# Sliding-window attention beside a GEGLU: three DMA queues by role, zero columns in front of v, a masked product, and an earlier x load

## The chip, the cores and the metric

The kernel runs on one core of a Trainium2 chip. The metric is the device time of one execution in microseconds (us). TensorE does matrix products into PSUM, VectorE and ScalarE work elementwise, GpSimd fills and prepares, and SyncE issues DMAs. DMAs can be issued from SyncE, from ScalarE and from GpSimd; each of the three has a queue of its own onto the core's 16 DMA engines.

## What is computed

x is 2048 x 512 in bfloat16. It is normalised over its rows, and the result xn goes two ways. One is attention with 32 heads of 16 columns, where each token looks at itself and at seven tokens before it, two apart; places before the first token are masked. The other is a GEGLU feed-forward network of width 1792. Their product, behind a SiLU, is added to x.

```python
qkv = xn @ wqkv                              # q, k, v: 32 heads x 16
idx = pos[:, None] - arange(8)[None, :] * 2  # tokens s, s-2, ... s-14
logits = einsum(q, k[idx]) * scale; logits = where(idx >= 0, logits, -1e9)
s = einsum(softmax(logits), v[idx]) @ wo
g = silu((gelu(xn @ w_gate) * (xn @ w_up)) @ w_down)
return x + s * g
```

## The kernel before, in words

The tokens are cut into four blocks j of 512. For each block the kernel normalises four tiles of 128 tokens (`layer_norm`: statistics L285 and L286, L317 the normalisation, all on VectorE; the reciprocal root for blocks 1 to 3 on GpSimd, L307 and L310), transposes them on TensorE (L333), and copies them into xnT (L339 on ScalarE, L341 on VectorE). `qkv` multiplies by wqkv in twelve column groups (L376), each into one of four PSUM buffers of ring "f"; ScalarE copies each to SBUF: q (L389), k (L391) and v (L396, tile vst, four buffers). A vst goes to DRAM at once, into vT_dram (L442, a DMA of SyncE), since the attention wants v in another layout: `load_values` reads it back (L467) as v_arr, with 32 heads x 4 offsets on the partitions. A block has two halves of four such DMAs each, so eight gathers; v_arr has three buffers. For block 0 the columns before the first token don't exist, so a GpSimd memset fills them (L461) and the DMA leaves them out.

`scores` multiplies q by shifted k on VectorE (L488, eight products a block), TensorE sums over the head's columns (L501), ScalarE takes the exponential (L513); in block 0 GpSimd memsets put zeros where a token has no predecessor (L518). `values` multiplies by v_arr (L598, eight products a block) and sums on TensorE (L612). `ffn_pair` computes gate and up (L659), GELU (L669) and their product (L676); `out_tile` does w_down (L713), wo (L701), the SiLU, the gate, the residual and the store (L737).

The order is fixed when the kernel is built. Every piece of work is a task with an engine, an estimated duration, what it depends on, which ring buffers it takes and frees, and a priority. The class Order places one task after another, always the one that could start first by these estimates (priority breaks ties), and so writes one order for each engine, which then executes its instructions strictly in that order. `x_there` and `w_there` are the estimated landing times of x and of the thirds of wqkv. TensorE's large products (`add_main`) are one chain.

DMAs before: SyncE loads half of block 0's x, the thirds of wqkv (L197) and x of blocks 1, 2, 3 (L201), then issues the stores of v, the gathers of v and the output stores, all in one queue. ScalarE loads the other half of block 0's x. GpSimd loads the four other weights (L802) in 14 DMAs, each batch behind the rstd of a block.

Of the kernel before, what the change touches and what calls it, by code (L numbers as in the profile page):

```python
# [9 lines left out]
ALU = mybir.AluOpType  # L10
AF = mybir.ActivationFunctionType
BF16 = mybir.dt.bfloat16
F32 = mybir.dt.float32

P = 128
H = 32
DH = 16
W = 8
PAD = 16
TQ = 512  # L20
HALO = 2 * (W - 1)
# [12 lines left out]
ACT1 = 0.62  # L34
# [9 lines left out]
class Order:  # L44
# [15 lines left out]
    def add(self, eng, dur, fn, deps=(), prio=0.0, takes=(), frees=(), func=None, opens=None, closes=None):  # L60
        t = Task()
        t.eng, t.dur, t.fn, t.prio = eng, dur, fn, prio
        t.deps = [d if isinstance(d, tuple) else (d, HOP) for d in deps if d is not None]
        t.takes, t.frees, t.func, t.opens, t.closes = takes, frees, func, opens, closes
        t.end = None
        t.seq = len(self.tasks)
        self.tasks.append(t)
        return t
# [61 lines left out]
def kernel(  # L130
# [11 lines left out]
    nc = tc.nc  # L142
    B, S, D = A_x.shape
    DF = B_w_gate.shape[1]
    NC = D // P
    NF = DF // P
    NJ = S // TQ
    TPB = TQ // P
    NT = S // P
    VL = TQ + 8  # L150
# [6 lines left out]
    cpool = pool("cpool", 1)  # L157
# [12 lines left out]
    dram = pool("dram", 1, space=bass.MemoryType.DRAM)  # L170
# [10 lines left out]
    add = order.add  # L181
# [5 lines left out]
    wo_sb = wpool.tile([P, NC, D], BF16, name="wo_sb")  # L187
    wg_sb = wpool.tile([P, NC, DF], BF16, name="wg_sb")
    wu_sb = wpool.tile([P, NC, DF], BF16, name="wu_sb")
    wd_sb = wpool.tile([P, NF, D], BF16, name="wd_sb")  # L190
    wqkv_v = A_wqkv.rearrange("(k p) n -> p k n", p=P)

    for t in range(TPB):
        eng = nc.sync if t % 2 == 0 else nc.scalar
        eng.dma_start(out=x_sb[:, t, :], in_=x2d[t * P : (t + 1) * P, :])  # L195
    for i in range(3):
        nc.sync.dma_start(  # L197
            out=wqkv_sb[:, :, i * D : (i + 1) * D], in_=wqkv_v[:, :, i * D : (i + 1) * D]
        )
    for j in range(1, NJ):  # L200
        nc.sync.dma_start(  # L201
            out=x_sb[:, j * TPB : (j + 1) * TPB, :],
            in_=x2d[j * TQ : (j + 1) * TQ, :].rearrange("(t p) d -> p t d", p=P),
        )
    x_there = [3.2, 3.5, 3.8, 4.1] + [9.5] * 4 + [11.5] * 4 + [13.5] * 4
    w_there = [6.0, 7.0, 8.0]


    warm = cpool.tile([P, TQ], BF16, name="warm")
# [45 lines left out]
    for q in range(4):  # L255
# [2 lines left out]
            in_=fold4[32 * q : 32 * (q + 1), :, :],  # L258
        )

    xnT = cpool.tile([P, NC, S], BF16, name="xnT")
    stats = cpool.tile([P, NT, nc.vector.BN_STATS_DIM], F32, name="stats")
    mv = cpool.tile([P, NT, nc.vector.BN_AGGR_DIM], F32, name="mv")
    rstd = cpool.tile([P, NT, 1], F32, name="rstd")
    vT_dram = dram.tile([D, S], BF16, name="vT_dram")
    tiles = {}


    warm_ps = psa.tile([P, TQ], F32, name="warm_ps", tag="a")
# [5 lines left out]
    copied = {}  # L275
    rstd_done = {}
# [121 lines left out]
    def qkv(j):  # L398
        for which in range(3):
            mms = []  # L400
            if j == 0:
                for half in range(2):
                    for c in range(NC):
                        ts = (2 * half, 2 * half + 1)
                        mms.append(
                            add_main(
                                2 * MM,
                                lambda c=c, half=half, which=which: qkv_mm(
                                    0, which, c, half * TQ // 2, (half + 1) * TQ // 2
                                ),  # L410
                                deps=[copied[t] for t in ts] + [(w_there[which], 0.0)],
                                takes=[("f", ("qkv", 0, which, c))] if half == 0 else [],
                            )
                        )
                mms = mms[NC:]
            else:
                for c in range(NC):
                    mms.append(
                        add_main(
                            4 * MM,  # L420
                            lambda c=c, which=which: qkv_mm(j, which, c, 0, TQ),
                            deps=[copied[t] for t in range(j * TPB, (j + 1) * TPB)],
                            takes=[("f", ("qkv", j, which, c))],
                        )
                    )
            for c in range(NC):
                takes = []
                if which == 0 and c == 0:
                    takes = [("q", j)]
                if which == 2:  # L430
                    takes = [("vst", (j, c))]
                e = add(
                    "act", ACT1, lambda c=c, which=which: qkv_evacuate(j, which, c), deps=[mms[c]],
                    prio=-0.5, takes=takes, frees=[("f", ("qkv", j, which, c))],
                )
                if which == 0:
                    q_ready[j] = e
                elif which == 1:
                    k_ready[j] = e
                else:  # L440
                    def store(c=c):
                        nc.sync.dma_start(  # L442
                            out=vT_dram[c * P : (c + 1) * P, j * TQ : (j + 1) * TQ],
                            in_=tiles["vst", j, c][:],
                        )

                    st = add("sp", 0.6, store, deps=[e], prio=-1.0, frees=[])

                    v_stored[j] = add(("dma", j, c), 2.6, lambda: None, deps=[(st, 0.0)], frees=[("vst", (j, c))])

    v_ready = {}

    def load_values(j, half):
        def fn():
            v_arr = vapool.tile([P, DH // 2, VL], BF16, name="v_arr")
            tiles["va", j, half] = v_arr
            for w4 in range(4):
                start = j * TQ - HALO + 2 * w4
                skip = max(0, -start)
                if skip:  # L460
                    nc.gpsimd.memset(v_arr[32 * w4 : 32 * (w4 + 1), :, 0:skip], 0.0)  # L461
                src = bass.AP(
                    tensor=vT_dram.tensor,
                    offset=vT_dram.offset + half * (DH // 2) * S + start + skip,
                    ap=[[S * DH, H], [S, DH // 2], [1, VL - skip]],
                )
                nc.sync.dma_start(out=v_arr[32 * w4 : 32 * (w4 + 1), :, skip:VL], in_=src)  # L467

        issue = add("sp", 2.2, fn, deps=[v_stored[j]], prio=0.0, takes=[("va", (j, half))])
        v_ready[j, half] = add(("dma", "va", j, half), 7.5, lambda: None, deps=[(issue, 0.0)])  # L470


# [3 lines left out]
    def scores(j, prio):  # L476
        exps = []
        for w2 in range(2):
# [30 lines left out]
            def expo(w2=w2):  # L509
                if w2 == 0:  # L510
                    tiles["attn", j] = atpool.tile([P, 2, TQ], BF16, name="attn", tag="attn")
                attn = tiles["attn", j]
                nc.scalar.activation(out=attn[:, w2, :], in_=tiles["L", j, w2][:], func=AF.Exp)  # L513
                if j == 0:
                    for w4 in range(4):
                        n = HALO - 2 * (w4 + 4 * w2)
                        if n > 0:
                            nc.gpsimd.memset(attn[32 * w4 : 32 * (w4 + 1), w2, 0:n], 0.0)  # L518

            ps = []  # L520
            for c in range(NC):
# [10 lines left out]
                "pe", COL16, reduce, deps=[ps[-1]], prio=-0.5, takes=[("a", ("L", j, w2))],  # L532
                frees=[("pr", ("S", j, w2, c)) for c in range(NC)],
            )
            exps.append(
                add(
                    "act", ACT1, expo, deps=[r], prio=-0.6, func="exp",
                    takes=[("attn", j)] if w2 == 0 else [], frees=[("a", ("L", j, w2))],
                )
            )  # L540

        def sums():
            s_ps = psa.tile([P, P], F32, name="sum_ps", tag="a")
# [30 lines left out]
            tiles["b", j] = atpool.tile([P, TQ], BF16, name="b_sb", tag="b_sb")  # L574
            nc.scalar.activation(out=tiles["b", j][:], in_=tiles["b_ps", j][:], func=AF.Copy)

        s = add("pe", 0.4, sums, deps=[(e, 0.5) for e in exps], prio=-0.4, takes=[("a", ("sum", j))])
        r = add("dve", 1.15, recip, deps=[s], prio=-1.5, frees=[("a", ("sum", j))])
        b = add("pe", 0.3, spread_back, deps=[r], prio=-0.4, takes=[("a", ("b", j))])
        b_ready[j] = add("act", ACT1, b_copy, deps=[b], prio=-0.6, frees=[("a", ("b", j))])  # L580
# [203 lines left out]
            add(("dma", "out", t, cs.start), 2.0, lambda: None, deps=[(st, 0.0)], frees=[("sg", t)] if end else [])  # L784


    def load_weights(j, prio):
        pieces = []
        if j == 1:
            v = B_w_gate.rearrange("(k p) n -> p k n", p=P)  # L790
            pieces = [(wg_sb[:, k, :], v[:, k, :]) for k in range(NC)]
        elif j == 2:
            v = B_w_up.rearrange("(k p) n -> p k n", p=P)
            pieces = [(wu_sb[:, k, :], v[:, k, :]) for k in range(NC)]
        else:

            v = A_wo.rearrange("(h g e) n -> e h g n", h=H, g=NC, e=4)
            pieces = [(wo_sb[32 * e : 32 * (e + 1), :, :], v[e]) for e in range(4)]
            v = B_w_down.rearrange("(k p) n -> p k n", p=P)
            pieces += [(wd_sb[:, k : k + 7, :], v[:, k : k + 7, :]) for k in range(0, NF, 7)]  # L800
        for o, i in pieces:
            add("pool", 1.0, lambda o=o, i=i: nc.gpsimd.dma_start(out=o, in_=i), deps=[rstd_done[j]], prio=prio)  # L802


    for j in range(NJ):
        layer_norm(j)
    for j in range(1, NJ):
        load_weights(j, 1.0 + j)
    for j in range(NJ):
        qkv(j)  # L810
    order.freed["h", "wqkv"] = 0.0
    for j in range(NJ):
        for half in range(2):
# [40 lines left out]
```

## Time and profile before

| what | us |
|---|---|
| median of 3 runs | 247.5 (246.55 to 248.46) |
| profiled execution | 246.81 |
| its span, first to last instruction | 245.1 |
| TensorE busy in the span | 229.6 |
| VectorE busy | 157.2 |
| ScalarE busy | 109.4 |
| GpSimd busy | 20.2 |

The profile is of one execution. Engines are called PE (TensorE), PEld (its weight loads), DVE (VectorE), ACT (ScalarE), POOL (GpSimd) and SP (SyncE); a q behind the name is the engine's queue, where DMAs are issued. L376 is line 376 of the kernel. Times are us from the start of the span unless marked ns. The span's 40 slices are 6.13 us each.

### The profile page before, as it was taken

What the parts mean: (1) busy time and instruction counts of PE and PEld (TensorE: products, weight loads), DVE (VectorE), ACT (ScalarE), POOL (GpSimd) and SP (SyncE); (2) the same over time, 40 slices, a digit from 0 to 9 for tenths busy, and PEclk for the clock granted to TensorE, in tenths of its full rate; (3) what the DMA queues carried; (4) which work ended last, traced back from release to release, by engine and by line L of the source; (5) the groups of instructions that cost most, each with busy time, mean ns of one, the idle gap of its engine ahead of it and who ended that gap; (6) DMA issues with size and microseconds to landing.
All of it is one profiled execution on the core that took longest, in us unless ns stands there. A gap on an engine that the chain in (4) does not pass through costs nothing.

```text
span 245.1 us, 3478 instructions
## 1 busy us (share of the span) xinstructions
PE 229.6 (94%) x1336; PEld 106.5 (43%) x1360; DVE 157.2 (64%) x232; ACT 109.4 (45%) x163; POOL 20.2 (8%) x58
## 2 busy tenths in 40 slices
PE   7879999819999999999999999999999999999992
PEld 2667543303444443444444444444444444444441
DVE  4699999934999999999998332233432333443131
ACT  2445567225784479671723341083233143335100
POOL 6057751000000000000000000000000000000000
PEclk9999999967999999999999999999999999999999
DMA  6929979959999800007300000100000100000001
GB/s 197 354 75 312 355 218 250 205 137 199 236 219 220 172 0 3 0 23 163 79 0 3 0 0 21 43 24 0 0 0 4 43 21 21 3 0 0 21 23 43
DMA packets 18529, 22.60 MB, mean 92 GB/s; under 512 B 1424, under 2 KB 17424, under 8 KB 18512
## 3 DMA queue, kind: packets, MB, share of 16 engines
q1 hardware_dynamic: 16912, 16.08, 27.3%
q0 software_dynamic: 1312, 6.03, 7.6%
q10 hardware_dynamic: 288, 0.26, 0.3%
q8 instruction: 10, 0.16, 0.3%
q14 instruction: 7, 0.06, 0.1%
HBM read 18.17 MB, written 4.19 MB: 91 GB/s over the span
## 4 chain that ended last, share of the span: by engine, by line
PE 86%; DMA 7%; DVE 3%; SPq 1%; issue 1%; ACT 1%; DVEq 0%; ACTq 0%
PE u_ps L659 20%; PE y_ps L713 20%; PE g_ps L659 20%; PE qkv_ps L376 13%; PE s_ps L701 6%; DMA vT_dram<-vst 3%; DMA x_sb<-in_A_x_dram 3%; PE L_ps L501 3%; PE O_ps L612 3%; DVE stats L285 2%; PE tr_ps L333 1%; SPq L197 1%; DVE mv L286 1%; SPq L195 0%; PE sum_ps L547 0%
## 5 line engine op out<-in xcount | busy, mean ns | idle before, releaser
L676 DVE TENSOR_TENSOR hT<-gl,u_ps 128x512 bf16<-128x512 bf16 x56 | 38.3, 686 | 36.6 <-PE u_ps L659 34.8
L659 PE MATMUL u_ps<-xnT,wu_sb 128*128 128x512 bf16 x220 | 57.0, 379 | 0.3
L659 PE MATMUL g_ps<-xnT,wg_sb 128*128 128x512 bf16 x217 | 56.5, 379 | 0.4 <-issue 0.2
L669 ACT ACTIVATE gl<-g_ps 128x512 bf16<-128x512 f32 x56 | 33.3, 597 | 49.8 <-PE g_ps L659 43.2
L376 PE MATMUL qkv_ps<-xnT,wqkv_sb 128*128 128x512 bf16 (+1 forms) x234 | 46.1, 344 | 7.5 <-ACT vst L396 6.3
L713 PE MATMUL y_ps<-wd_sb,hT 128*128 128x512 bf16 x217 | 50.3, 379 | 0.4
L598 DVE TENSOR_TENSOR pv<-attn,v_arr 128x2048 bf16<-128x2048 bf16 x32 | 37.8, 1220 | 7.1 <-PE L_ps L501 6.6
L488 DVE TENSOR_TENSOR prod<-q_sb,k_sb 128x2048 bf16<-128x2048 bf16 x32 | 37.6, 1220 | 0.0
L659 PEld LDWEIGHTS <-wg_sb 128*128 128x128 bf16 x224 | 21.6, 98 | 27.2 <-issue 1.7
L376 PEld LDWEIGHTS <-wqkv_sb 128*128 128x128 bf16 x240 | 22.7, 99 | 24.7 <-issue 10.9
L659 PEld LDWEIGHTS <-wu_sb 128*128 128x128 bf16 x224 | 21.5, 98 | 27.0 <-issue 1.7
L713 PEld LDWEIGHTS <-hT 128*128 128x128 bf16 x224 | 21.7, 98 | 26.2 <-issue 0.4
L727 DVE TENSOR_TENSOR sg<-sil,s_ps 128x512 bf16<-128x512 bf16 (+1 forms) x17 | 11.0, 655 | 34.2 <-PE s_ps L701 22.9
L724 ACT ACTIVATE sil<-y_ps 128x512 bf16<-128x512 f32 x16 | 9.6, 597 | 43.8 <-PE y_ps L713 43.8
L701 PE MATMUL s_ps<-wo_sb,o_sb 128*128 128x512 bf16 (+1 forms) x68 | 16.4, 366 | 0.0
L396 ACT ACTIVATE vst<-qkv_ps 128x512 bf16<-128x512 f32 x16 | 9.0, 599 | 15.8 <-DMA vT_dram<-vst 8.3
L285 DVE BATCH_NORM_STATS2 stats<-x_sb 128x6 f32<-128x512 bf16 x16 | 10.8, 673 | 3.7 <-DMA x_sb<-in_A_x_dram 3.7
L391 ACT ACTIVATE k_sb<-qkv_ps 128x512 bf16<-128x512 f32 x16 | 9.2, 599 | 4.6 <-PE qkv_ps L376 4.6
L389 ACT ACTIVATE q_sb<-qkv_ps 128x512 bf16<-128x512 f32 x16 | 8.9, 602 | 5.0 <-PE qkv_ps L376 5.0
L701 PEld LDWEIGHTS <-o_sb 128*128 128x128 bf16 x68 | 6.6, 98 | 7.2
L623 ACT ACTIVATE o_sb<-O_ps 128x1024 bf16<-128x1024 f32 x8 | 8.2, 1022 | 2.1 <-PE O_ps L612 1.5
L669 ACT ACT_TABLE_LOAD x7 | 9.0, 1283 | 0.1
(56 smaller groups left out, 116.6 us busy)
## 6 DMA issues: line engine op xcount, KB each, us to landing
v_arr<-vT_dram SPq DMA_DIRECT2D x24, 260.0 KB, 5.5
vT_dram<-vst SPq DMA_DIRECT2D x16, 128.0 KB, 6.3
out_dram<-sg SPq DMA_DIRECT2D x15, 128.0 KB, 1.7
wg_sb<-in_B_w_gate_dram POOLq DMA_DIRECT2D x4, 448.0 KB, 4.9
wu_sb<-in_B_w_up_dram POOLq DMA_DIRECT2D x4, 448.0 KB, 9.2
wd_sb<-in_B_w_down_dram POOLq DMA_DIRECT2D x2, 896.0 KB, 9.7
wqkv_sb<-in_A_wqkv_dram SPq DMA_DIRECT2D x3, 512.0 KB, 6.2
x_sb<-in_A_x_dram SPq DMA_DIRECT2D x3, 512.0 KB, 8.8
```

The lines of the kernel that those rows point to most:

```text
L285: nc.vector.bn_stats(out=stats[:, t, :], in_=x_sb[:, t, :])
L376: nc.tensor.matmul(tiles["qkv", j, fo][:, lo:hi], lhsT=wqkv_sb[:, dk, fo * P : (fo + 1) * P], rhs=xnT[:, dk, j * TQ + lo : j * TQ + hi], s ...
L391: nc.scalar.activation(out=k_sb[:, c, PAD + j * TQ : PAD + (j + 1) * TQ], in_=ps[:], func=AF.Copy)
L488: nc.vector.tensor_tensor(out=prod[:], in0=tiles["q", j][:, c, :].unsqueeze(1).to_broadcast([P, 4, TQ]), in1=kwin, op=ALU.mult,)
L598: nc.vector.tensor_tensor(out=pv[:], in0=tiles["attn", j][:, w2, :].unsqueeze(1).to_broadcast([P, 4, TQ]), in1=tiles["va", j, half][:, 4 * ...
L659: nc.tensor.matmul(ps[:], lhsT=w[:, dk, fc * P : (fc + 1) * P], rhs=xnT[:, dk, j * TQ : (j + 1) * TQ], start=(dk == 0), stop=(dk == NC - 1),)
L669: nc.scalar.activation(out=tiles["gl", j, fc][:], in_=tiles["g_ps", j, fc][:], func=AF.Gelu_apprx_tanh)
L676: nc.vector.tensor_tensor(out=tiles["h", j][:, fc, :], in0=tiles["gl", j, fc][:], in1=tiles["u_ps", j, fc][:], op=ALU.mult,)
L701: nc.tensor.matmul(tiles["s", t][:, cs], lhsT=tiles["o", j][:, c, tt * P : (tt + 1) * P], rhs=wo_sb[:, c, cs], start=(c == 0), stop=(c == ...
L713: nc.tensor.matmul(tiles["y", t][:], lhsT=tiles["h", j][:, fc, tt * P : (tt + 1) * P], rhs=wd_sb[:, fc, :], start=(fc == 0), stop=(fc == N ...
L724: nc.scalar.activation(out=tiles["sil", t][:], in_=tiles["y", t][:], func=AF.Silu)
L727: nc.vector.tensor_tensor(out=tiles["sg", t][:, cs], in0=tiles["sil", t][:, cs], in1=tiles["s", t][:, cs], op=ALU.mult,)
```

## The change

Four things, in one edit. The DMAs are split over queues by role: SyncE keeps the loads of x and wqkv, the stores of v and the output; the gathers of v are issued by GpSimd; the four other weights are issued by ScalarE, in seven larger DMAs, each behind a certain copy of ScalarE's. The DRAM copy of v gets 16 columns of zeros in front, written once by a GpSimd DMA, so that block 0 gathers like the others and needs no fills. The first tokens' places are set to zero by a VectorE product with a mask (built once by GpSimd) in place of GpSimd memsets. SyncE's load of x of block 1 moves ahead of the last third of wqkv. The planner's estimates are changed to go with it.

```diff
+    load_wqkv(0)
+    load_wqkv(1)
+    load_x(1)
+    load_wqkv(2)
+    load_x(2)
+    load_x(3)
-    x_there = [3.2, 3.5, 3.8, 4.1] + [9.5] * 4 + [11.5] * 4 + [13.5] * 4
-    w_there = [6.0, 7.0, 8.0]
+    x_there = [3.2, 3.5, 3.8, 4.1] + [10.0] * 4 + [13.0] * 4 + [16.0] * 4
+    w_there = [7.0, 8.5, 11.5]
...
+    vT_dram = dram.tile([D, PAD + S], BF16, name="vT_dram")
+    nc.gpsimd.dma_start(
+        out=vT_dram[:, 0:PAD].rearrange("(c p) n -> p c n", p=P), in_=k_sb[:, :, 0:PAD]
+    )
+    mask = cpool.tile([P, 2, PAD], BF16, name="mask")
+    nc.gpsimd.memset(mask[:], 1.0)
+    for w4 in range(4):
+        for w2 in range(2):
+            n = HALO - 2 * (w4 + 4 * w2)
+            if n > 0:
+                nc.gpsimd.memset(mask[32 * w4 : 32 * (w4 + 1), w2, 0:n], 0.0)
...
-                start = j * TQ - HALO + 2 * w4
-                skip = max(0, -start)
-                if skip:
-                    nc.gpsimd.memset(v_arr[32 * w4 : 32 * (w4 + 1), :, 0:skip], 0.0)
...
-                nc.sync.dma_start(out=v_arr[32 * w4 : 32 * (w4 + 1), :, skip:VL], in_=src)
-        issue = add("sp", 2.2, fn, deps=[v_stored[j]], prio=0.0, takes=[("va", (j, half))])
+                    offset=vT_dram.offset + half * (DH // 2) * SP + PAD + j * TQ - HALO + 2 * w4,
+                    ap=[[SP * DH, H], [SP, DH // 2], [1, VL]],
+                nc.gpsimd.dma_start(out=v_arr[32 * w4 : 32 * (w4 + 1), :, :], in_=src)
+        issue = add("pool", 2.4, fn, deps=[v_stored[j]], prio=-2.0, takes=[("va", (j, half))])
...
-                if j == 0:
-                    for w4 in range(4):
-                        n = HALO - 2 * (w4 + 4 * w2)
-                        if n > 0:
-                            nc.gpsimd.memset(attn[32 * w4 : 32 * (w4 + 1), w2, 0:n], 0.0)
+            def masked(w2=w2):
+                a = tiles["attn", j][:, w2, 0:PAD]
+                nc.vector.tensor_tensor(out=a, in0=a, in1=mask[:, w2, :], op=ALU.mult)
...
+            if j == 0:
+                e = add("dve", 0.1, masked, deps=[e], prio=-1.5)
...
-        s = add("pe", 0.4, sums, deps=[(e, 0.5) for e in exps], prio=-0.4, takes=[("a", ("sum", j))])
+        s = add("pe", 0.4, sums, deps=[(e, 0.3) for e in exps], prio=-0.4, takes=[("a", ("sum", j))])
...
-    def load_weights(j, prio):
...
-            add("pool", 1.0, lambda o=o, i=i: nc.gpsimd.dma_start(out=o, in_=i), deps=[rstd_done[j]], prio=prio)
+    def load_weights():
+        def load(o, i):
+            return lambda: nc.scalar.dma_start(out=o, in_=i)
+        def start(o, i, dep):
+            add("act", 0.5, load(o, i), deps=[dep], prio=-3.0)
+        start(wg_sb[:], B_w_gate.rearrange("(k p) n -> p k n", p=P), copied[2])
+        start(wu_sb[:], B_w_up.rearrange("(k p) n -> p k n", p=P), k_ready[1])
+        v = A_wo.rearrange("(h g e) n -> e h g n", h=H, g=NC, e=4)
+        for e in range(4):
+            start(wo_sb[32 * e : 32 * (e + 1), :, :], v[e], k_ready[2])
+        start(wd_sb[:], B_w_down.rearrange("(k p) n -> p k n", p=P), q_ready[3])
```

## Rows read from the trace of the kernel before

**Rows 1.** The page's 40 slices, busy tenths of TensorE and VectorE.

```profile
PE   7879999819999999999999999999999999999992
...
DVE  4699999934999999999998332233432333443131
```

**Rows 2.** Who waited for whom: us in total, times, longest us.

```profile
ACT vst L396 <- DMA vT_dram<-vst: 8.3, 1, 8.3
...
PE qkv_ps L376 <- ACT vst L396: 6.3, 1, 6.3
```

**Rows 3.** Windows: length, busy us (instructions) of each engine, clock, DMA share, GB/s.

```profile
core 0: us, PE busy (x) PEld busy (x) DVE busy (x) ACT busy (x) POOL busy (x), PEclk, DMA share, GB/s
...
47.90:54.20 6.30, 0.01 (x2) 0.00 (x1) 3.25 (x3) 0.65 (x2) 0.00 (x0) 0.73 0.74 172
...
54.20:57.70 3.50, 3.50 (x9) 0.99 (x8) 0.00 (x0) 2.01 (x4) 0.00 (x0) 0.50 0.55 136
```

**Rows 4.** Timeline of ScalarE, the v copies: start, us, instruction, idle before.

```profile
30.79 0.60 ACT L396 ACTIVATE vst<-qkv_ps 128x512 bf16<-128x512 f32 x1 [0.77 <-PE qkv_ps L376]
...
34.17 1.24 ACT L396 ACTIVATE vst<-qkv_ps 128x512 bf16<-128x512 f32 x2 [1.93 <-PE L_ps L501]
...
53.55 2.06 ACT L396 ACTIVATE vst<-qkv_ps 128x512 bf16<-128x512 f32 x4 [8.29 <-DMA vT_dram<-vst]
...
66.62 0.60 ACT L396 ACTIVATE vst<-qkv_ps 128x512 bf16<-128x512 f32 x1 [0.32 <-PE qkv_ps L376]
```

**Rows 5.** Timeline of SyncE's queue: gathers of block 0, stores of block 1.

```profile
34.87 5.57 SPq L467 DMA_DIRECT2D v_arr<-vT_dram  x8
45.26 4.05 SPq L442 DMA_DIRECT2D vT_dram<-vst  x4
```

**Rows 6.** DMA issues running at 34.9, 39.7, 20.6-22.8, 56.4-59.0, 32.8-33.6: us to landing.

```profile
v_arr<-vT_dram SPq DMA_DIRECT2D x1, 253.0 KB, 10.3
...
v_arr<-vT_dram SPq DMA_DIRECT2D x1, 256.0 KB, 13.6
...
vT_dram<-vst SPq DMA_DIRECT2D x4, 128.0 KB, 11.2
...
vT_dram<-vst SPq DMA_DIRECT2D x4, 128.0 KB, 6.2
...
wd_sb<-in_B_w_down_dram POOLq DMA_DIRECT2D x1, 896.0 KB, 12.0
```

**Rows 7.** Timeline around block 1's first normalisation.

```profile
9.45 0.60 ACT L339 ACTIVATE xnT<-tr_ps 128x512 bf16<-128x512 bf16 x1 [1.42 <-PE tr_ps L333]
...
14.64 0.66 DVE L285 BATCH_NORM_STATS2 stats<-x_sb 128x6 f32<-128x512 bf16 x1
...
17.02 1.03 DVE L317 TENSOR_SCALAR xn_t<-x_sb,mv,rstd 128x512 bf16<-128x512 bf16 x3
...
17.46 0.40 PE L333 MATMUL tr_ps<-ident,xn_t 128*128 128x128 bf16 x4 [1.27 <-DVE xn_t L317]
```

**Rows 8.** The chain that ended last: the load of x of block 1.

```profile
3.28 8.12 DMA x_sb<-in_A_x_dram
```

**Rows 9.** DMA issues by line: ns min/median/max, first and last start.

```profile
L802 POOL DMA_DIRECT2D wo_sb<-in_A_wo_dram x4: 550/632/710, 28.3 to 31.1; - x4
L802 POOL DMA_DIRECT2D wd_sb<-in_B_w_down_dram x2: 1009/1026/1042, 31.8 to 32.7; - x2
...
L467 SPq DMA_DIRECT2D v_arr<-vT_dram x32: 302/444/1546, 34.9 to 111.9; - x32
```

**Rows 10.** Timeline: gathers of the third and fourth half, products with v.

```profile
60.58 7.93 SPq L467 DMA_DIRECT2D v_arr<-vT_dram  x8
...
67.35 5.77 DVE L598 TENSOR_TENSOR pv<-attn,v_arr 128x2048 bf16<-128x2048 bf16 x5
```

**Rows 11.** GpSimd's power product of rstd: ns min/median/max.

```profile
L310 POOL TENSOR_TENSOR rstd<-rstd,mhalf x3: 1045/1048/1858, 15.2 to 26.5; 128x4 f32<-128x4 f32 x3
```

**Rows 12.** VectorE by line: the cast, busy us, mean ns, idle before.

```profile
L559 DVE CAST rs<-rs 128x128 bf16<-128x128 f32 x4 | 0.9, 227 | 0.1
```

**Rows 13.** DMA issues running at 60.5-62.5: KB each, us to landing.

```profile
v_arr<-vT_dram SPq DMA_DIRECT2D x4, 260.0 KB, 5.8
```

More of the change, by code (lines that the diff above doesn't have):

```diff
@@ L195, with load_wqkv @@
         eng.dma_start(out=x_sb[:, t, :], in_=x2d[t * P : (t + 1) * P, :])
-    for i in range(3):
+    def load_wqkv(i):
         nc.sync.dma_start(
@@ L199, with load_x @@
         )
-    for j in range(1, NJ):
+    def load_x(j):
         nc.sync.dma_start(
@@ L259 @@
         )
+    tiles = {}
+    vT_dram = dram.tile([D, PAD + S], BF16, name="vT_dram")
[9 more added lines that the diff above has]
+                nc.gpsimd.memset(mask[32 * w4 : 32 * (w4 + 1), w2, 0:n], 0.0)
     xnT = cpool.tile([P, NC, S], BF16, name="xnT")
@@ L264 @@
     rstd = cpool.tile([P, NT, 1], F32, name="rstd")
-    vT_dram = dram.tile([D, S], BF16, name="vT_dram")
-    tiles = {}
     warm_ps = psa.tile([P, TQ], F32, name="warm_ps", tag="a")
@@ L442, in store @@
                         nc.sync.dma_start(
-                            out=vT_dram[c * P : (c + 1) * P, j * TQ : (j + 1) * TQ],
+                            out=vT_dram[c * P : (c + 1) * P, PAD + j * TQ : PAD + (j + 1) * TQ],
                             in_=tiles["vst", j, c][:],
@@ L447, in qkv @@
                     st = add("sp", 0.6, store, deps=[e], prio=-1.0, frees=[])
-                    v_stored[j] = add(("dma", j, c), 2.6, lambda: None, deps=[(st, 0.0)], frees=[("vst", (j, c))])
+                    v_stored[j] = add(("dma", j, c), 3.0, lambda: None, deps=[(st, 0.0)], frees=[("vst", (j, c))])
     v_ready = {}
@@ L456, in fn @@
             tiles["va", j, half] = v_arr
+            SP = PAD + S
             for w4 in range(4):
-                start = j * TQ - HALO + 2 * w4
-                skip = max(0, -start)
-                if skip:
-                    nc.gpsimd.memset(v_arr[32 * w4 : 32 * (w4 + 1), :, 0:skip], 0.0)
                 src = bass.AP(
                     tensor=vT_dram.tensor,
-                    offset=vT_dram.offset + half * (DH // 2) * S + start + skip,
-                    ap=[[S * DH, H], [S, DH // 2], [1, VL - skip]],
-                )
-                nc.sync.dma_start(out=v_arr[32 * w4 : 32 * (w4 + 1), :, skip:VL], in_=src)
-        issue = add("sp", 2.2, fn, deps=[v_stored[j]], prio=0.0, takes=[("va", (j, half))])
+                    offset=vT_dram.offset + half * (DH // 2) * SP + PAD + j * TQ - HALO + 2 * w4,
+                    ap=[[SP * DH, H], [SP, DH // 2], [1, VL]],
+                )
+                nc.gpsimd.dma_start(out=v_arr[32 * w4 : 32 * (w4 + 1), :, :], in_=src)
+        issue = add("pool", 2.4, fn, deps=[v_stored[j]], prio=-2.0, takes=[("va", (j, half))])
         v_ready[j, half] = add(("dma", "va", j, half), 7.5, lambda: None, deps=[(issue, 0.0)])
@@ L534, in scores @@
             )
[L535 to L539, printed above, removed]
-            )
+            e = add(
+                "act", ACT1, expo, deps=[r], prio=-0.6, func="exp",
+                takes=[("attn", j)] if w2 == 0 else [], frees=[("a", ("L", j, w2))],
+            )
+            if j == 0:
+                e = add("dve", 0.1, masked, deps=[e], prio=-1.5)
+            exps.append(e)
         def sums():
@@ L784, in out_tile @@
             add(("dma", "out", t, cs.start), 2.0, lambda: None, deps=[(st, 0.0)], frees=[("sg", t)] if end else [])
-    def load_weights(j, prio):
[L788 to L801, printed above, removed]
-            add("pool", 1.0, lambda o=o, i=i: nc.gpsimd.dma_start(out=o, in_=i), deps=[rstd_done[j]], prio=prio)
+    def load_weights():
[9 more added lines that the diff above has]
+        start(wd_sb[:], B_w_down.rearrange("(k p) n -> p k n", p=P), q_ready[3])
     for j in range(NJ):
         layer_norm(j)
-    for j in range(1, NJ):
-        load_weights(j, 1.0 + j)
     for j in range(NJ):
         qkv(j)
+    load_weights()
     order.freed["h", "wqkv"] = 0.0
```

## The prediction

> **What bounds the kernel now.** I read the page's 40 slices first. TensorE is nearly solid but for one hole, in the slice that begins near 49 us, while VectorE is full before and behind it [rows 1]. The view of waits names the hole: TensorE waits 6.3 us, once, for the ScalarE copy of v (L396), and that copy waited 8.3 us for the transfer of an earlier vst to DRAM [rows 2]. So four vst buffers were full, the copy could not free its PSUM buffer, and TensorE had no fourth one to go on with. The windows give its price in two parts: in 47.9 to 54.2 TensorE was busy 0.01 of 6.30 us, and in the 3.50 us behind it the granted clock was 0.50, that is 1.2 instead of 2.4 GHz [rows 3].
>
> Why was the vst not away? Block 1's four v copies began at 30.79 and ended at 35.41 us [rows 4], but SyncE issued their stores only from 45.26, behind eight gathers that it had begun at 34.87 [rows 5]. The first gather landed 10.3 us after its issue, at 45.2, and there the first store goes; the eighth, whose issue ran at 39.7, landed 13.6 us after it, at about 53, some eight microseconds after that store went [rows 5, 6]. So a store doesn't wait for all that read the same DRAM tensor. I read it as a limit of eight transfers in flight on one queue: the ninth goes when the first lands. It is order on SyncE's queue, and a queue for the stores alone removes it.
>
> **The change part by part.** Sums are made against the profiled execution, 246.81 us: the span of 245.1 and 1.7 around it. The median of the runs shown is 247.5, 0.7 above it.
>
> *Stores alone on SyncE, gathers to GpSimd.* The 6.30 us go and so do 3.50 x 0.50 = 1.75 us of half clock: **-8.05 us**. What is late next is the stores' landing. Block 1's first copy ends at 31.39; for the copy that needs its buffer to end by 47.9 (0.65 us with its release) it may take 15.9 us. The next wait of this kind is a block later: block 2's copies began at 53.55, block 3's at 66.62 [rows 4], 13.1 us apart; take off 1.75 us of half clock, add the 2.0 us by which TensorE's wait was shorter than ScalarE's [rows 2], take off the copy's 0.6: a store may take 12.7 us. Stores beside gathers took 6.2 us, stores beside the weights 11.2 [rows 6]. After the change gathers and weights lie in two other queues, but only one weight matrix is moving while block 1 stores; I take 9 us, and both allowances hold.
>
> The first lesson against this: the Trainium skill, "DMA: Bandwidth & Descriptors", section "Issuing engines are not separate DMA queues", says that all queues end on the same 16 engines and interleave, and that issuing from several saves only the issue time. By it nothing would be gained if the hole were bandwidth; the trace says that the stores weren't issued at all for ten to fourteen microseconds, which the rule doesn't speak of. Its interleaving is what the third rival below is made of.
>
> *x of block 1 ahead of the last third of wqkv.* It landed at 11.40 [rows 8]; VectorE then made statistics of seven tiles, four of block 1 and three of block 2, before block 1's first normalisation at 17.02, and TensorE waited 1.27 us for that [rows 7]. So at best this gains 1.27. Against it: the whole w_gate now starts on ScalarE's queue right behind the copy of tile 2, which ended at 10.05 [rows 7], when x of blocks 2 and 3 is still loading. It is 1.75 MB, and VectorE takes its instructions in order: the first statistics of block 2, at 14.64 [rows 7], stand before block 1's normalisation. The two transfers can share evenly for as long as x of block 2 has left, so 0 to 3 us later. The 512 pieces of 32 B that put zeros in front of v fall here too; x of block 1 was the fourth load of 512 pieces in a row and landed 8.12 us after its issue [rows 8], so 512 pieces, far larger ones, take about 2 us: 0 to 2, inside the same bounds. Bounds -1.27 to +3; I take 0.
>
> *Masks.* Seven short GpSimd fills go, two VectorE products of 128x16 elements come. No such form is in the trace; the nearest small VectorE instruction is the 128x128 cast at 0.227 us [rows 12]. Two cost 0 to 0.45 us, in the slices of 34 to 43 us, where VectorE is full [rows 1]. Being in order they also make the products behind them wait for the exponential. Bounds 0 to 2; I take +0.3.
>
> *Gathers issued by GpSimd.* 32 issues at 0.55 to 1.04 us (its loads now, [rows 9]) against 0.30 to 1.55 on SyncE. The 14 weight loads leave GpSimd, and the fills too. One place is exposed: if the order puts block 0's eight gathers (4.4 to 8.3 us) before GpSimd's rstd of block 3, the normalisation behind it holds VectorE; the planner counts 4.8 us of that, so 0 to 3.5 unplanned. I take +0.3. The ring of three v_arr buffers has its own place: block 1's second half was issued at 60.58 when a buffer came free, landed some 5.8 us after issue, so about 68.4, and its use came behind four of the five products that began at 67.35, at 72.0 [rows 10, 13]. 3.6 us of slack against 0.4 to 2.4 us more of issue: 0, with w_down beside it perhaps 2; I take +0.2.
>
> The second lesson: the Trainium skill, "SBUF — State Buffer", section "Summary: rules for kernel authors", advises against hiding a GpSimd DMA under VectorE, since its descriptors are starved; the page has 620 ns become 3100. By that estimate each gather would issue in some 3 us. The trace doesn't bear this out for the products of this kernel: the wo loads, issued between 28.3 and 31.1 us with products running, took 0.55 to 0.71 [rows 9]. What it does show is a GpSimd product stretched from 1.05 to 1.86 us beside VectorE's [rows 11]; that is the second rival.
>
> *Weights issued by ScalarE.* Seven issues at 0.30 to 1.55 us (SyncE's gathers as the nearest hardware queue [rows 9]), 2 to 11 us of ScalarE's time over 50. Four of them, wo, come right behind block 2's last k copy, near the old hole; TensorE's tolerance of 2.0 us covers four short ones (1.2 to 1.8 us), not four long ones. Bounds 0 to 4; I take +0.2.
>
> Sum: 246.81 - 8.05 + 0 + 0.3 + 0.3 + 0.2 + 0.2 = 239.8; with the 0.7 to the median of runs, **240.4 us**.
>
> **Rivals.** (1) *The order stays, in another form*: the limit in flight is not SyncE's own, and the stores still wait behind gathers. For it: only SyncE's queue is seen at the limit. Against it: a w_down load of GpSimd's was in flight beside the eight gathers, nine in all: issued before 33.6, it took 12.0 us [rows 6]. Time: about 247. (2) *GpSimd becomes late.* At the ratio 1.86/1.05 the planned 4.8 us of block 0's issues last 8.5, so rstd of block 3 and with it VectorE are 3.7 late, and block 1's second half loses another 2 behind its slack: 240.4 + 5.7 = 246. For it: VectorE is full from 20 us on, so nothing absorbs it; against it the wo rows. (3) *The other side, slower: stores crawl between long packets of two other queues.* The stores' slowing beside weights (11.2) and beside gathers (6.2) adds up rather than one taking the place of the other, and GpSimd's gathers go in longer packets. It decides from 17.4 us a store: there the two overruns (17.4 - 15.9 and 17.4 - 12.7) and one half-clock stretch of 1.75 have eaten the 8.05. At 20 us: 4.1 + 7.3 + 2 x 1.75 - 8.05 = +6.9, so about 254 with the small terms on top left out. For it: 11.2 us were already seen with one competitor. Against it: w_up, 1.75 MB, is the only matrix moving then. (4) *Start and ScalarE at their bad ends*: +3 and +4 in place of 0 and 0.2, hence 247.
>
> **How the numbers follow.** The forecast 0.66; rival 1 0.05; rival 2 0.09; rival 3 0.11; rival 4 0.09. About 1% (2.5 us) is what a measurement of this kernel can tell from no change. Faster by over 1% is under 245: all of the forecast, and the milder part (0.04) of rivals 2 and 4: 0.70. Slower is over 250: rival 3 and the worst sums of the others, 0.12. The rest, 0.18, lies within. Range: below, 240.4 less 1.27 of the start, the 1.0 of small terms and a rounding for the order's new places, 236.5; above, rivals 1, 2 and 4 are taken in and rival 3 left out: 247.5.
>
> **What would show it.** Right: no wait of TensorE for L396 over 1 us, the clock at 1.00 through 43 to 70, block 1's stores issued within 1 us of their copies and landing in under 12, FFN matmuls from about 62 instead of 70 us. GpSimd's gathers at 0.6 to 1.0 us each, L802's issues on ScalarE under 0.6. Wrong: stores of 15 us and more; VectorE waiting for v_arr or for rstd in the middle; TensorE's first transposes of block 1 later than 18 us; ScalarE held over 2 us by an issue.

## The result, and the profile after

The changed kernel takes 240.3 us (median of four executions, 240.06 to 244.24) beside 247.2 us for the kernel before on the same chip: a ratio of 0.972, interval 0.968 to 0.976. Measured once more among the experiments it took 241.3 us, ratio 0.980 (0.973 to 0.986). The forecast was 240.4.

Ratios leave out executions over 1.5% longer than the kernel's fastest, such as the 244.24 us here, whose loads of x landed late, and two of 619 and 1364 us among the experiments. That of 244.24 us is the one profiled with the result, so the rows here are of the second measurement's profile, 241.78 us with a span of 240.1, against 245.1 before.

The page's slices of the kernel after (second measurement), TensorE and VectorE:

```profile
PE   7799999999978998999999999999999999999992
...
DVE  4899999999489999994669943333432144343131
```

The empty slice of [rows 1] near 49 us is full. What is left is a dent of TensorE (7, 8) in the two slices from 66 to 78 us, with one of VectorE just ahead of it (4, 8). The view of waits of the same execution says what the dent is:

```profile
DVE pv L617 <- DMA v_arr<-vT_dram: 3.7, 1, 3.7
...
PE g_ps L678 <- DVE hT L695: 1.8, 1, 1.8
...
PE O_ps L631 <- DVE pv L617: 1.1, 1, 1.1
```

No row says that TensorE or the copy of v (now L418) waits for a store: both rows of [rows 2] are gone. Instead VectorE waits once for a gather of v, until 66.65 us, and TensorE behind it for 2.9 us in two pieces. The windows of the same execution, columns as in [rows 3]:

```profile
8.00:24.00 16.00, 15.92 (x151) 13.11 (x153) 14.91 (x43) 8.80 (x16) 3.03 (x5) 1.00 0.73 259
43.00:54.00 11.00, 10.95 (x90) 4.35 (x84) 10.97 (x12) 7.20 (x14) 4.16 (x8) 1.00 0.92 231
54.00:70.00 16.00, 14.12 (x89) 5.93 (x89) 12.23 (x13) 10.45 (x15) 5.22 (x9) 1.00 1.04 269
70.00:86.00 16.00, 14.59 (x99) 5.93 (x100) 16.00 (x18) 9.59 (x13) 2.32 (x4) 1.00 0.54 121
```

The clock is 1.00 in all four, where [rows 3] had 0.50. From 54 to 86 TensorE is idle for 1.88 + 1.41 = 3.3 us: the dent. In the start, 8 to 24, it is busy 15.92 us; the same window of the kernel before:

```profile
8.00:24.00 16.00, 14.52 (x140) 12.14 (x142) 13.56 (x40) 7.72 (x16) 7.92 (x16) 1.00 0.72 232
```

So the change has a second gain, 1.4 us of start; TensorE's wait of 1.27 us ahead of block 1's transposes [rows 7] is gone. Three more rows of the kernel after: stores of v from 28 to 64 us with their landing, gathers and wo's issues (ns min/median/max, first and last start):

```profile
L464 SPq DMA_DIRECT2D vT_dram<-vst x12: 319/320/636, 29.4 to 61.2; - x12
...
DMA to landing us min/median/max: 6.2/9.8/12.2
...
L486 POOL DMA_DIRECT2D v_arr<-vT_dram x32: 584/587/667, 23.5 to 101.7; - x32
...
L808 ACTq DMA_DIRECT2D wo_sb<-in_A_wo_dram x4: 603/615/662, 41.6 to 43.6; - x4
```

Block 1's first store goes at 29.4 us, where it went at 45.26 [rows 5].

### The profile page after: what moved, and what is told of

It reads as the page before. It is cut to its first block, busy times and chain, and to the rows that moved or that the text cites. A ratio compares the mean times of both kernels' runs of the same rounds, so it can differ in the third digit from the quotient of the medians.

```text
span 242.5 us, 3469 instructions
## 1 busy us (share of the span) xinstructions
PE 228.9 (94%) x1337; PEld 106.0 (44%) x1360; DVE 157.1 (65%) x234; ACT 108.6 (45%) x162; POOL 30.2 (12%) x70
## 3 DMA queue, kind: packets, MB, share of 16 engines
q0 software_dynamic: 2592, 8.54, 15.9%
## 4 chain that ended last, share of the span: by engine, by line
PE 78%; DVE 9%; DMA 6%; issue 2%; SPq 2%; DVEq 0%
PE y_ps L732 20%; PE u_ps L678 17%; PE g_ps L678 17%; PE qkv_ps L398 13%; DMA x_sb<-in_A_x_dram 6%; PE s_ps L720 6%; DVE prod L507 4%; PE O_ps L631 3%; PE L_ps L520 2%; DVE hT L695 2%; SPq L203 1%; DVE pv L617 1%; PE tr_ps L355 1%; SPq L198 1%; PE b_ps L584 1%
## 5 line engine op out<-in xcount | busy, mean ns | idle before, releaser
L695 DVE TENSOR_TENSOR hT<-gl,u_ps 128x512 bf16<-128x512 bf16 x56 | 38.2, 684 | 33.6 <-PE u_ps L678 28.0
L398 PE MATMUL qkv_ps<-xnT,wqkv_sb 128*128 128x512 bf16 (+1 forms) x234 | 44.4, 336 | 3.2 <-DVE xnT L363 1.8
L398 PEld LDWEIGHTS <-wqkv_sb 128*128 128x128 bf16 x240 | 22.2, 98 | 20.2 <-issue 2.1
L486 POOL DMA_DIRECT2D v_arr<-vT_dram x32 | 18.7, 589 | 62.2 <-DVE pv L617 37.5
L418 ACT ACTIVATE vst<-qkv_ps 128x512 bf16<-128x512 f32 x16 | 9.1, 603 | 4.8 <-PE qkv_ps L398 4.7
```

The source lines that it names most:

```text
L398: nc.tensor.matmul(tiles["qkv", j, fo][:, lo:hi], lhsT=wqkv_sb[:, dk, fo * P : (fo + 1) * P], rhs=xnT[:, dk, j * TQ + lo : j * TQ + hi], s ...
L486: nc.gpsimd.dma_start(out=v_arr[32 * w4 : 32 * (w4 + 1), :, :], in_=src)
L695: nc.vector.tensor_tensor(out=tiles["h", j][:, fc, :], in0=tiles["gl", j, fc][:], in1=tiles["u_ps", j, fc][:], op=ALU.mult,)
```

## The experiments

Each kernel was timed in three rounds beside the kernel before.

**The same kernel again.**

> The changed kernel as it is, for a profile to set beside the others. Both theories: 240 to 241 us; no wait of TensorE for a v copy over 1 us. If the 242.5 us span of the profile on record is the kernel's own, the span is 242 again; if the late x of block 3 (landing at 21.6 us) was an accident of that execution, it lands before 20 us and the span is about 238.5.

241.26 us (240.06 to 241.95). Its rows are those above: x of block 3 landed at 14.1 us (21.6 in the profile of the execution of 244.24 us), and the span was 240.1, not 238.5.

**The hole: one queue less for the stores.** The kernel before, with nothing but v's stores moved from SyncE to ScalarE:

```diff
-                        nc.sync.dma_start(
+                        nc.scalar.dma_start(
...
-                    st = add("sp", 0.6, store, deps=[e], prio=-1.0, frees=[])
+                    st = add("act", 0.35, store, deps=[e], prio=-1.0, frees=[])
```

> The kernel before with one thing changed: the stores of v are issued by ScalarE right behind their copies, on its own queue; gathers, weights, fills and the x order stay. Queue theory (block 1's stores stand behind gathers in flight on SyncE's queue): block 0's stores still take 8 to 12 us beside the weights, but block 1's go at once, no wait of TensorE for a v copy over 1 us, 239 to 242 us. Rival (the late landing of block 0's stores is enough for the hole): the hole stays at 4 us or more, 245 us and up.

241.41 us, ratio 0.983 (0.973 to 0.992), span 240.5. The timeline of ScalarE shows each copy of block 1 and its store right behind it:

```profile
30.48 0.60 ACT L396 ACTIVATE vst<-qkv_ps 128x512 bf16<-128x512 f32 x1 [0.71 <-PE qkv_ps L376]
31.11 0.33 ACTq L442 DMA_DIRECT2D vT_dram<-vst  x1
```

TensorE no longer waits for vst. The gathers are as many and as large as before, on the queue where they were: the hole was order, not bandwidth, and within the intervals this one edit gives what the whole change gives. By the span it gives 4.6 us and not 8.05. A part of the rest can be placed: TensorE, busy 15.95 of 16 us from 70 to 86 before, loses 1.4 us there, behind a VectorE that has idled 2.2 us:

```profile
70.00:86.00 16.00, 14.54 (x98) 5.91 (x98) 16.00 (x18) 9.54 (x13) 0.00 (x0) 1.00 0.71 131
```

```profile
DVE pv L598 <- PE O_ps L612: 2.2, 1, 2.2
```

VectorE's product starts at 66.33 us. The last gather that it needs was issued only at 62.26 and landed at 66.15, by the trace, so the wait is read here as one for that gather and not for O_ps (argued, not tested); why it was issued so late is told under "Only the weights moved".

**The other half of the same cure: only the gathers moved to GpSimd.**

```diff
-                nc.sync.dma_start(out=v_arr[32 * w4 : 32 * (w4 + 1), :, skip:VL], in_=src)
+                nc.gpsimd.dma_start(out=v_arr[32 * w4 : 32 * (w4 + 1), :, skip:VL], in_=src)
...
-        issue = add("sp", 2.2, fn, deps=[v_stored[j]], prio=0.0, takes=[("va", (j, half))])
+        issue = add("pool", 2.4, fn, deps=[v_stored[j]], prio=-2.0, takes=[("va", (j, half))])
```

> The kernel before with one thing changed: the gathers of v are issued by GpSimd; weights, fills, masks and the x order stay as before. Queue theory (block 1's stores stand behind gathers still in flight on SyncE's queue): stores go within 1 us of their copies, the 6.3 us hole and the half clock go, 239 to 241.5 us. Rival (the hole comes from the weights that slow block 0's stores and so everything behind them): those stores still take 11 to 12 us, the hole stays at 4 us or more, 244 to 247 us.

248.84 us, ratio 1.011 (1.006 to 1.015): slower than before, with the hole gone. From its view of waits:

```profile
PE tr_ps L333 <- DVE xn_t L317: 7.6, 3, 4.7
DVE xn_t L317 <- POOL rstd L310: 5.2, 1, 5.2
```

and its timeline of GpSimd:

```profile
33.60 0.63 POOL L467 DMA_DIRECT2D v_arr<-vT_dram  x1 [9.37 <-DMA vT_dram<-vst]
```

GpSimd takes its instructions in order. It stood 9.4 us for block 0's stores, then issued eight gathers, and only then came to rstd of block 3, for which VectorE waited 5.2 and TensorE 4.7 us. This is the prediction's second rival, from order rather than from slow issues.

**The same, with the gathers told to come behind rstd of block 3.**

```diff
-        issue = add("pool", 2.4, fn, deps=[v_stored[j]], prio=-2.0, takes=[("va", (j, half))])
+        issue = add("pool", 2.4, fn, deps=[v_stored[j], rstd_done[NJ - 1]], prio=-2.0, takes=[("va", (j, half))])
```

> The run with the gathers alone on GpSimd, and in GpSimd's order the rstd of block 3 stands ahead of block 0's gathers. If that run lost its gain to VectorE's 5.2 us wait for the rstd behind the gathers, this one has no such wait and 240 to 243 us. Rival (GpSimd's gathers cost something else, in the transfers or at VectorE): 245 us and up although the wait is gone.

249.13 us, ratio 1.009 (1.004 to 1.014). The wait for rstd is gone and another is there, in its waits:

```profile
PE sum_ps L547 <- POOL attn L518: 6.1, 1, 6.1
```

and in the timeline of GpSimd (two of its rows):

```profile
43.35 0.99 POOL L802 DMA_DIRECT2D wd_sb<-in_B_w_down_dram  x1 [0.72 <-DMA v_arr<-vT_dram]
...
48.88 0.35 POOL L518 MEMSET attn<- 32x6 bf16 x3
```

The fills that set block 0's first tokens to zero now stand behind DMA issues of GpSimd that wait. In the kernel before they were done by 41.2 us.

**The same, with the fills turned into VectorE products** (`masked` and `mask` of the change; the weights stay on GpSimd, v_arr's columns are still filled, the order of x is the old one):

```diff
-                        if n > 0:
-                            nc.gpsimd.memset(attn[32 * w4 : 32 * (w4 + 1), w2, 0:n], 0.0)
+            def masked(w2=w2):
+                a = tiles["attn", j][:, w2, 0:PAD]
+                nc.vector.tensor_tensor(out=a, in0=a, in1=mask[:, w2, :], op=ALU.mult)
```

> The kernel before with gathers on GpSimd behind rstd of block 3 (as the last run of that pair) and, new, block 0's first tokens masked by two VectorE products; weights stay on GpSimd, v_arr's columns are still filled. Theory (the mask is a needed part: the fills stood in GpSimd's order behind gathers and weight issues that wait): the 6.1 us wait of TensorE at sum_ps for GpSimd's attn is gone, no wait for vst either, clock 1.00 through 43 to 54, 240 to 243 us, ratio about 0.98. Rival (the gathers' own lateness, not the fills, held TensorE): a wait of 4 us or more comes back at the next place, pv for v_arr, and the time stays 246 to 249.

241.31 us, ratio 0.977 (0.968 to 0.986). Its windows:

```profile
8.00:24.00 16.00, 13.20 (x130) 11.35 (x132) 12.22 (x34) 7.07 (x14) 6.80 (x12) 1.00 0.71 222
43.00:54.00 11.00, 10.68 (x90) 4.57 (x91) 10.78 (x12) 7.19 (x14) 4.32 (x6) 1.00 1.03 286
54.00:70.00 16.00, 15.89 (x110) 6.67 (x111) 15.88 (x17) 11.84 (x17) 6.94 (x12) 1.00 1.04 251
70.00:86.00 16.00, 15.87 (x106) 6.56 (x107) 16.00 (x19) 9.47 (x13) 2.31 (x4) 1.00 0.59 121
```

From 43 us on TensorE is full, without the dent of the changed kernel: w_down is issued earlier here, at 43.4 and 44.6 us. What it lacks against the changed kernel is the start, 13.20 us in place of 15.92. The zero columns in front of v are not in this kernel, so the gain doesn't need them; they were not tried alone.

**And the products taken out of the change**: the kernel after, with the seven fills on GpSimd again (the same lines, the other way round).

> The kernel after with the first tokens of block 0 filled by GpSimd again in place of VectorE's products. Theory (the product is a needed part): the last three fills stand in GpSimd's order behind four gathers of block 1 that wait for its stores to land at 43 us; with 2.4 us of issue they come at about 46 us where the changed kernel's sums begin at 39.4, TensorE waits 3 to 7 us at sum_ps for attn, half clock behind it, 244 to 248 us. Rival (the products only cost VectorE 0.3 us, as predicted): 240.5 to 241.5, no wait at sum_ps.

248.89 us, ratio 1.011 (1.007 to 1.016): without the products the change is worth nothing. Its waits, then its timeline of GpSimd:

```profile
PE sum_ps L558 <- POOL attn L530: 6.9, 1, 6.9
```

```profile
43.77 2.40 POOL L479 DMA_DIRECT2D v_arr<-vT_dram  x4 [10.12 <-DMA vT_dram<-vst]
46.21 0.35 POOL L530 MEMSET attn<- 32x6 bf16 x3
```

Four gathers wait 10.1 us for block 1's stores to land, and the last three fills stand behind them. TensorE waits 6.9 us for 0.35 us of fills, with a mean clock of 0.59 from 43 to 54 us (1.00 in the changed kernel). An order with the fills ahead of these gathers was not tried.

**Only the weights moved**: the kernel before with the change's seven weight loads on ScalarE (`load_weights` of the change).

> The kernel before with one thing changed: the four weights are issued early by ScalarE in seven DMAs; SyncE's queue keeps loads, stores and gathers in the order of before. New theory (the early w_gate gets out of the way of block 0's stores, so its gathers are half landed when block 1's stores come): block 0's stores land within 3 us, no wait of TensorE for a v copy over 1.5 us, 239 to 242 us, the whole gain by this part alone. Rival (it needs the queue split, or the zero columns and masks, as well): 243 to 247 us.

246.53 us, ratio 1.001 (0.996 to 1.005): no difference. Its waits:

```profile
DVE pv L598 <- DMA v_arr<-vT_dram: 6.4, 1, 6.4
...
PE u_ps L659 <- DVE hT L676: 3.7, 1, 3.7
```

and those of SyncE's queue:

```profile
SPq L442 <- DMA wo_sb<-in_A_wo_dram: 10.7, 1, 10.7
SPq L467 <- DMA wd_sb<-in_B_w_down_dram: 9.4, 1, 9.4
```

The hole is gone here as well: block 0's stores no longer run beside the weights, its gathers issue from 24.2 us in place of 34.87 [rows 5], and block 1's stores find them landed. But two DMAs of SyncE now stood for transfers that ScalarE had issued and whose data they don't touch. The compiled program's own list of waits shows why (instruction, and the semaphore that it waits for):

```
L789 DMA wd_sb<-in_B_w_down_dram 128x14x512 [waits DMAHW2_49]
L467 DMA v_arr<-vT_dram 32x8x520 [waits DMAHW2_49]
```

Eight completion semaphores (DMAHW0 to 7) go round the DMAs of SyncE and ScalarE, in the program's order, and each DMA waits for the one that had its semaphore before. The gather behind w_down has w_down's: it was issued at 63.81, w_down landed at 63.80. The trace has the same by number: 100, 102 to 104 and 107 to 110 for SyncE and ScalarE, and in the kernels where GpSimd issues DMAs, 111 to 118 for these, a set of eight of their own. In the run with the stores on ScalarE it is the late gather's reason too: issued at 62.26, with the semaphore of a store of ScalarE's that landed at 62.24.

**Only the weights, with w_down late**: issued behind the fifth GELU of block 0.

```diff
-        start(wd_sb[:], B_w_down.rearrange("(k p) n -> p k n", p=P), q_ready[3])
...
+        if (j, fc) == (0, 4):
+            wd_v = B_w_down.rearrange("(k p) n -> p k n", p=P)
+            add("act", 0.5, lambda: nc.scalar.dma_start(out=wd_sb[:], in_=wd_v), deps=[a], prio=-3.0)
```

> The kernel before with the weights on ScalarE early, as in the run with this alone, but w_down issued behind the fifth GELU of block 0. Gathers stay on SyncE. Theory (transfers of SyncE and ScalarE share eight places in flight, and w_down held the gathers of block 1's second half for 9.7 us): these gathers issue one behind the other from 54 us, VectorE's wait of 6.4 us for v_arr falls under 1, 239.5 to 242 us. Rival (they wait for something else of SyncE's queue): the wait stays over 4 us and the time at 245 to 247.

239.1 to 241.34 us in three executions, ratio 0.972 (0.963 to 0.981), as the theory has it. No row of this kernel is read, so that the wait for v_arr went is inferred from the time alone.

**The change with the gathers back on SyncE** (the lines of the second experiment's diff, reversed).

> The changed kernel with one thing undone: the gathers of v are on SyncE's queue again, the weights stay early on ScalarE's. Queue theory: block 0's stores land by 24 us as in the changed kernel, so its gathers are issued some ten microseconds earlier than before the change and are half landed when block 1's stores come at 32.8; the hole is under 1.5 us and the time 240 to 243 us. Rival (any gather ahead of the stores on one queue makes the hole, however early): TensorE waits 4 us or more for a v copy, 244 to 247 us.

240.66 us, ratio 0.978 (0.971 to 0.984), the same as the whole change, and TensorE doesn't wait for a v copy. SyncE's queue still has its waits on w_down and wo:

```profile
SPq L464 <- DMA wo_sb<-in_A_wo_dram: 11.5, 1, 11.5
SPq L486 <- DMA wd_sb<-in_B_w_down_dram: 7.8, 1, 7.8
```

From 54 to 86 us they cost TensorE nothing; the dent of the change isn't there:

```profile
54.00:70.00 16.00, 15.89 (x110) 6.72 (x110) 15.89 (x17) 11.76 (x17) 0.00 (x0) 1.00 0.96 252
70.00:86.00 16.00, 15.89 (x106) 6.51 (x106) 16.00 (x19) 9.74 (x14) 0.00 (x0) 1.00 0.99 203
```

**The change with w_down late** (the edit shown above, made in the kernel after).

> The changed kernel with w_down issued behind a GELU of block 0 in place of block 3's q. If w_down in flight beside the gathers of block 1's second half makes VectorE's 2.6 to 3.7 us wait for v_arr, and that TensorE's waits of 1.8 and 1.1 us near 70, all of these go and the time is 1.5 to 3 us less, 237.5 to 239.5. Rival (those gathers are late by GpSimd's issue or the buffer ring alone): the wait stays over 2 us, 240 to 241.5.

238.45 us (238.02 to 240.14), ratio 0.970 (0.963 to 0.978), span 236.3. Its windows:

```profile
8.00:24.00 16.00, 15.94 (x151) 13.10 (x153) 14.91 (x43) 8.80 (x16) 3.00 (x5) 1.00 0.73 256
43.00:54.00 11.00, 10.95 (x91) 4.37 (x85) 10.97 (x12) 7.23 (x14) 4.16 (x8) 1.00 0.80 202
54.00:70.00 16.00, 15.89 (x110) 6.65 (x109) 15.91 (x18) 11.21 (x16) 5.56 (x10) 1.00 0.99 228
70.00:86.00 16.00, 15.89 (x108) 6.67 (x103) 16.00 (x18) 11.53 (x14) 1.91 (x4) 1.00 0.74 183
```

The dent is gone, 0.22 us of idle TensorE from 54 to 86 in place of 3.3. The DMA issues between 50.5 and 54.5 us (KB each, us to landing), first of the kernel after, then of this one:

```profile
wd_sb<-in_B_w_down_dram ACTq DMA_DIRECT2D x1, 1792.0 KB, 16.7
v_arr<-vT_dram POOLq DMA_DIRECT2D x4, 260.0 KB, 11.5
```

```profile
v_arr<-vT_dram POOLq DMA_DIRECT2D x4, 260.0 KB, 5.1
```

Gathers of GpSimd don't share w_down's semaphores, and they were issued at the same times in both kernels, 52.2 to 54.0 us; here it was the traffic itself, which made them land 6.4 us later (medians).

**w_gate late too**: the last kernel with `q_ready[0]` in place of `copied[2]` for w_gate.

> The kernel after with w_down behind the fifth GELU of block 0 and w_gate behind block 0's q copies (about 13 us in place of 9.3). Theory (w_gate beside x of blocks 2 and 3 is worth little in an ordinary execution, since TensorE has no wait there): 237 to 238.5 us, within 0.5% of the version with w_down alone; x of block 3 lands at 13 instead of 14 us. Rival (w_gate's share of the start costs a microsecond or more): under 237.

238.50 us (238.0 to 239.01), ratio 0.966 (0.960 to 0.972): the same. x of block 3 landed at 14.0 us as before, not at 13. w_gate beside x of blocks 2 and 3 costs nothing that can be measured.

**The order of x back**: the kernel after with the old order of SyncE's loads.

> The changed kernel with one thing undone: x of block 1 behind the last third of wqkv again, with the old estimates of landing. My prediction's term of 0 for this part: within 1 us of the changed kernel, 239.3 to 241.3. Rival (the earlier x is worth the 1.27 us wait ahead of block 1's transposes): 241.3 to 242.

Ratio 0.979 (0.969 to 0.990), from two executions, 239.97 and 242.07 us: the same as the change itself. So the time doesn't tell what the order is worth, and in the profile the loads landed late, TensorE busy 12.98 us from 8 to 24. Rows of the other kernels say more, where the first third of wqkv landed by 7 us: 14.5 to 14.8 us busy in that window with the old order (the kernel before, only the stores moved, only the weights moved), 15.9 with the new (the change again, fills back, w_down late, w_gate late too). That is 1.1 to 1.4 us, across kernels that differ in other things as well. Where it landed at 7.8 us or later the window read 13.0 to 13.6 with the old order, 15.3 and 13.0 with the new; x of block 3 landed anywhere from 14.0 to 21.6.

This profile shows the shared semaphores once more. Two rows of its waits:

```profile
ACT attn L532 <- DMA wu_sb<-in_B_w_up_dram: 5.4, 1, 5.4
...
PE qkv_ps L398 <- ACT vst L418: 2.3, 1, 2.3
```

The fourth load of wo has w_up's semaphore. w_up took 18.8 us here and landed at 49.73, the load was issued at 49.76, and ScalarE stood for it with the v copy behind. In the change again the same load had 0.6 us to spare (issued at 43.60, w_up landed at 42.97): a late w_up can bring part of the hole back.

## Why the prediction was right, and where not

**The hole: right.** -8.05 was the term. With the dent removed the span falls from 245.1 to 236.3, by 8.8: the 8.05 and the 1.4 of the start, less 0.65 of small losses that are not placed. No run has the term by itself: the stores moved alone gave 4.6, with another wait behind them. For the estimate of 9 us for a store's landing 9.8 was measured (median), and no wait came of it; even with the late loads of the last run no store took over 15.1. The third rival (from 17.4 us on) did not come about. TensorE's first FFN matmul comes at 60.3 us (forecast: about 62, from 70), GpSimd's gathers issue in 0.58 to 0.67 us, ScalarE's single loads in under 0.4 and wo's in 0.60 to 0.66, a little over the 0.6 named.

**Its reason: half right.** "I read it as a limit of eight transfers in flight on one queue" was the step. Eight is right; one queue is not. In the kernel before, block 1's first two stores went at 45.26 and 46.44 us, and the gathers with their semaphores had landed at 45.19 and 46.38. But the semaphores of SyncE and ScalarE go round together, so that a queue "for the stores alone" is only free if what the other engine issues lands early. The first rival said just that ("the limit in flight is not SyncE's own"); it did not come about since the gathers went to GpSimd, whose semaphores are its own, and ScalarE's weights had landed when their semaphores came round: the nine that were seen in flight were eight and one. Where w_up had not landed, in the last run, ScalarE was held 5.4 us by an issue, one of the prediction's signs of being wrong.

**w_down: wrong by an order of magnitude.** "With w_down beside it perhaps 2; I take +0.2" was the mis-sized term, and VectorE's wait for v_arr is one of the prediction's signs of being wrong. It costs 3.3 - 0.22 = 3.1 us by TensorE's windows, 2.8 by the medians (241.26 to 238.45; 1.9 from the first measurement's 240.34). The intervals of the ratios, 0.973 to 0.986 and 0.963 to 0.978, overlap, so the size rests on the windows. Both numbers for it were at hand: the slack of 3.6 us, and stores that took 11.2 us beside weights against 6.2 beside gathers. By them a gather late by 6.4 us overruns 3.6 by 2.8. In the kernels themselves the last of the four gathers landed at 59.87 us with w_down late and 66.57 with it beside; its product could begin at 63.0, so the slack was 3.1 and the overrun 3.6. The prediction weighed the rows for stores and not for gathers.

**The start: wrong by 1.4 the other way.** 0 was taken from bounds of -1.27 to +3; the good end came. The two misses nearly cancel: 246.81 - 8.05 - 1.4 + 0.3 + 2.8 = 240.5. That the total was met so closely is luck; that it fell by a good 2% is not.

**The masks: the cost right, the meaning missed.** Two products of 0.15 us are the +0.3 that was taken. But they were priced as a cost alone. They are what makes gathers on GpSimd possible: with fills, in the order that the planner then makes, the change takes 248.9 us, some 8 more. The prediction named GpSimd's order as a risk for rstd only ("I take +0.3": no such wait in the change, but 5.2 us where the gathers were moved alone), and did not ask which other instructions of GpSimd TensorE would wait for.

On the Trainium skill's "DMA: Bandwidth & Descriptors", section "Issuing engines are not separate DMA queues": that several issuers save issue time alone doesn't cover the hole, which moving the stores to another issuer removed, with the traffic unchanged; that all queues interleave on the same engines agrees with w_down, beside which the gathers' landing went from 5.1 to 11.5 us. On "SBUF — State Buffer", section "Summary: rules for kernel authors": it has a GpSimd DMA starved of descriptors under VectorE in its 2x and 4x modes. No row names VectorE's mode, but the gathers issued at 0.58 to 0.67 us while VectorE was busy 10.97 of 11 us, so none was starved here.

## What to carry to other kernels

Before a slow or waiting instruction is moved to an in-order engine, list everything else that this engine still does for others: a 0.35 us fill behind a gather that waits for its data cost 7 us, and two products of 0.15 us on VectorE took its place. Where a DMA waits for a transfer whose data it doesn't need, look at which completion semaphores the program deals out, and to which engines together. A large load that nobody needs for long should be issued behind the transfers that someone waits for, not beside them: w_down, first used at 95.7 us, issued at 69.4 in place of 50.9 was worth about 1%, on top of the change.

## What the runs showed that was not expected

The one-edit kernel (v's stores from ScalarE, 241.4 us) is as fast as the whole change (240.3 and 241.3); the best version is the change with w_down behind a GELU (238.5, with w_gate later too or not). Three ways of clearing SyncE's queue all removed the hole, and two of them, each alone, gave the whole gain back in another place: 1.011 with the gathers moved, 1.001 with the weights. The small stores pay more for company than the gathers, which went from 5.1 to 11.5 us. Block 0's four stores, with only the end of w_gate beside the first two (the DMA issues of the kernel after between 18 and 28 us, in the profile taken with the result):

```profile
vT_dram<-vst SPq DMA_DIRECT2D x4, 128.0 KB, 1.7
```

1.7 us to landing, and 6.2 to 12.2 for the later ones of the change again, of the same size, beside gathers and weights.
